# Second-layer token tiles placed between the block products of the next pair, and remainders of h computed a step later

## The chip, the core and the metric

The kernel runs on one core of a Trainium2 chip. Its engines work side by side, each through its own queue in order: TensorE (PE; its weight loads are listed as PEld), VectorE (DVE), ScalarE (ACT), GpSimd (POOL) and the engine that issues transfers (SP). The metric is the device time of one execution in microseconds (us).

## The reference

```python
x = attention(q, k, v)                  # window of 128 positions; 1152 tokens x 512
out = 0
for e in range(4):                      # four experts, 512 -> 1024 -> 512, every token
    h = np.maximum(x @ w1[e], 0.0)
    out += p[:, e:e + 1] * (h @ w2[e])
h = np.maximum(out @ w_in, 0.0)         # 512 -> 2048 -> 512
return h * h @ w_out
```

All is float32. The kernel splits each operand into a rounded high part and a remainder (`xh`, `xl`; `wh`, `wl`) and forms three products for each one: high by high, high by remainder, remainder by high.

## The kernel before

The work stands in the program in this order: attention; expert 0 and half of expert 1 (a planner sets the order, then a loop over items); the **pair stage**; and the last two weight matrices, handled as two more experts of 1024 (`e` of 4 and 5). An item is one slice of hidden features for one chunk of tokens. The change touches the pair stage, 20 items called pairs: the second half of expert 1 and experts 2 and 3, in slices `g` of 256 features, for two chunks of tokens (`PAIRS`). Chunk 0 has 2 x 256 tokens and chunk 1 has 2 x 320. The order is expert, then two slices, then chunk, then slice: (1,0,2), (1,0,3), (1,1,2), (1,1,3), (2,0,0) and so on, as (expert, chunk, slice). They are numbered 1 to 20 here.

`gemm1_pair` computes a pair's first layer as 2 x 2 blocks with seven block products instead of eight. Sums of weight blocks (`hs`, `ls`) and of token blocks (`ht`, `lt`, `hm`, `lm`) have been made ahead. A block product is six matmuls with 256 or 320 columns (2 parts of the contraction by 3), so a pair has 42. They accumulate in three PSUM tiles `pa`, `pb`, `pc`. Results of one product are read from PSUM before the next product is added to the same tile: DVE's `u2` reads `pb` after the second product, and the fifth product goes into `pb` again; `u3` reads it after the fifth, and the seventh goes into it.

`relu` makes the two parts of h for a quarter of the pair: ACT writes the high part, DVE the remainder (line 973). Three quarters come from sums c12, c21 (DVE) and c22 (POOL, line 1001).

`flush_one` computes the second layer of a pair that is pending. For each tile of 128 tokens (4 for chunk 0, 5 for chunk 1) `gemm2_pair` issues six matmuls with 512 columns into a `yacc` tile of PSUM. There are five such banks, taken in turn. After the second of two slices, `evac` (line 1063, DVE) adds each finished tile to y. In the main loop the flush of pair n-1 follows the seven products of pair n as one block:

```python
h = gemm1_pair(e, ch, f)
...
if len(pend) > (1 if two else LAG):
    flush_one()
```

`fill` is called between the products and between the tiles. It hands out steps of the background work on ACT, DVE and POOL: splitting later weights (line 347, and lines 199 to 214 for the last matrices, whose split is longer). `run_x2` transposes finished y tiles into the next `xh` and `xl`: four PE transposes into a PSUM tile of the `work` kind (the kind of `pa`, `pb`, `pc`; three banks in turn), an ACT copy (line 1082) and a DVE subtraction (line 1083). Before, one such tile follows each of the first four tiles of the flush of pair 19.

Of the kernel before, what the change touches and what calls it, by code (L numbers as in the profile page):

```python
# [13 lines left out]
ALU = mybir.AluOpType  # L14
# [116 lines left out]
def kernel(  # L131
# [814 lines left out]
    def gemm1_pair(e, ch, g):  # L946
# [23 lines left out]
        def relu(i, j, src):  # L970
            hh, hl = (x[:, j * n:(j + 1) * n] for x in h[i])
            nc.scalar.activation(out=hh, in_=src, func=ACTF.Relu)  # L972
            nc.vector.scalar_tensor_tensor(  # L973
                out=hl, in0=src, scalar=0.0, in1=f32(hh), op0=ALU.max, op1=ALU.subtract
            )

        p1, p5, u2, u3, c12, c21, c22 = (
            tmp(x) for x in ("p1", "p5", "u2", "u3", "c12", "c21", "c22")
        )
# [4 lines left out]
        add(u2, pb, p1)  # L984
        fill(0.6, step)
# [4 lines left out]
        relu(0, 0, pa)  # L990
        mm(pb, s3, f["t3"], False, False)
        add(u3, pb, p1)
        fill(0.6, step)
        mm(pc, s4, f["b22"], False, True)
        add(c12, pc, u2)
        relu(0, 1, c12)
        fill(0.6, step)
        mm(pb, a22, f["m4"], False, True)
        add(c21, pb, p1)
        relu(1, 0, c21)  # L1000
        nc.gpsimd.tensor_tensor(out=c22, in0=u3, in1=p5, op=ALU.add)  # L1001
        spent("POOL", 0.9)
        relu(1, 1, c22)
        fill(0.6, step)
        return h
# [138 lines left out]
    def flush_one():  # L1144
        e, ch, f, h, two = pend.pop(0)
        if two:
            first, last = f % 2 == 0, f % 2 == 1
        else:
            n = FT // 2 if e in (1, E) else FT
            first, last = f % n == 0, f % n == n - 1  # L1150
# [3 lines left out]
        for tile_ in ys[e, ch]:  # L1154
            if two:
                gemm2_pair(e, ch, f, h, tile_, first, last)
            else:
                gemm2(e, ch, f, h, [tile_], first, last)
            if last:
                evac(e, ch, [tile_], f, two)  # L1160
            elif two:
                run_x2()
            fill(1.0, 1.38 if two else 0.69)
        w_done(w2t, e, ch, f, two)
        if last:
            tiles = ys.pop((e, ch))
            if e == E - 1 and f == NQ - 1:
                x2todo.extend(PAIRS[ch][0] // P + i for i, _ in tiles)

# [390 lines left out]
    for it, (e, ch, f, two) in list(enumerate(items))[N1:]:  # L1560
# [8 lines left out]
        if two:  # L1569
            assert ch < len(PAIRS) - 1 or not xbg  # L1570
            h = gemm1_pair(e, ch, f)
# [8 lines left out]
        if two and not (pend or [(0, 0, 0, 0, two)])[0][4]:  # L1580
            while pend:
                flush_one()
# [11 lines left out]
        if len(pend) > (1 if two else LAG):  # L1594
# [43 lines left out]
```

## Time and profile before

| | us |
|---|---|
| median of three runs | 683.14 (683.11 to 684.08) |
| the profiled execution | 684.94 |
| its span, first to last instruction | 682.5 |
| pair stage in that span | 228.55 to 474.51 |
| PE busy in the span | 670.5 |

The profiled execution is 1.80 us above the median. Its span leaves out 2.44 us of its own time. The granted clock of TensorE was full in the whole pair stage.

### The profile page before, as it was taken

How to read it: one execution, taken by the hardware profiler on the slowest of the kernel's cores; microseconds unless marked ns; L12 is line 12 of the kernel's file. 1: busy time of each engine (PE TensorE's matmuls, PEld its weight loads, DVE VectorE, ACT ScalarE, POOL GpSimd, SP SyncE). 2: the span in 40 equal slices, each digit the busy share in tenths (PEclk: the TensorE clock that was granted, in tenths of full speed). 3: DMA queues.
4: the chain of work that ended last, by engine and by line, in shares of the span. 5: the costliest groups of instructions: out<-in, count | busy, mean ns of one | idle time of the engine just before them, and what ended most of it. 6: DMA issues, size and time to landing. Idle time of an engine off the chain costs nothing.

```text
span 682.5 us, 10267 instructions
## 1 busy us (share of the span) xinstructions
PE 670.5 (98%) x3792; PEld 596.8 (87%) x3792; DVE 415.4 (61%) x885; ACT 296.7 (43%) x697; POOL 286.5 (42%) x297
## 2 busy tenths in 40 slices
PE   8999999999999999999999999999999999999997
PEld 7777888889999898999899898888999999989996
DVE  4897898855556445444563557887777688742121
ACT  5798787633222323222323233333555544432221
POOL 2799996515443455334555433010322222222221
PEclk7999999999999999999999999999999999999999
DMA  7933222030300112101101203147204200001011
GB/s 204 280 104 96 70 77 62 11 124 31 122 5 29 32 32 93 62 32 40 54 32 61 63 1 124 61 162 259 74 4 168 76 0 1 1 1 47 1 46 46
DMA packets 37106, 47.60 MB, mean 70 GB/s; under 512 B 3392, under 2 KB 25408, under 8 KB 37056
## 3 DMA queue, kind: packets, MB, share of 16 engines
q1 hardware_dynamic: 37056, 46.95, 22.0%
q8 instruction: 29, 0.48, 0.3%
q14 instruction: 21, 0.17, 0.1%
HBM read 44.58 MB, written 2.36 MB: 69 GB/s over the span
## 4 chain that ended last, share of the span: by engine, by line
PE 87%; DVE 4%; POOL 3%; ACT 2%; issue 1%; SPq 1%; DMA 1%; POOLq 0%; ACTq 0%
PE hps L858 24%; PE yacc L1045 24%; PE yacc L1013 16%; PE hps L958 15%; PE xps L653 3%; PE tp L781 2%; PE sc L733 1%; POOL wl L422 1%; POOL ts L769 1%; DMA pt<-in_probs_dram 1%; PE hps L1454 1%; DVE y L1063 1%; SPq L1278 1%; POOL vl L422 1%; PE xtp L1078 1%
## 5 line engine op out<-in xcount | busy, mean ns | idle before, releaser
L1045 PE MATMUL yacc<-wh,hmem 128*128 128x512 f32 x488 | 165.8, 393 | 0.0
L1034 POOL TENSOR_TENSOR hmem<-r,hmem 128x384 fp32r<-128x384 f32 x48 | 53.1, 1106 | 161.1 <-ACT hmem L1033 158.9
L858 PE MATMUL hps<-xh,wh 128*128 128x384 f32 (+1 forms) x352 | 115.8, 329 | 0.0
L1013 PE MATMUL yacc<-wh,hmem 128*128 128x512 f32 x360 | 115.2, 391 | 0.0
L858 PE MATMUL hps<-xh,wl 128*128 128x384 f32 (+1 forms) x352 | 114.4, 325 | 0.4 <-DVE wl L347 0.4
L858 PE MATMUL hps<-xl,wh 128*128 128x384 f32 (+1 forms) x352 | 113.9, 324 | 0.0
L1045 PEld LDWEIGHTS yacc<-wh,hmem 128*128 128x128 f32 x488 | 91.6, 188 | 17.4
L1045 PE MATMUL yacc<-wl,hmem 128*128 128x512 f32 x244 | 96.2, 394 | 0.0
L1013 PEld LDWEIGHTS yacc<-wh,hmem 128*128 128x128 f32 x360 | 67.6, 188 | 13.5
L1013 PE MATMUL yacc<-wl,hmem 128*128 128x512 f32 x180 | 70.2, 390 | 0.0
L858 PEld LDWEIGHTS hps<-xh,wh 128*128 128x128 f32 x352 | 66.3, 188 | 3.6 <-issue 0.2
L858 PEld LDWEIGHTS hps<-xl,wh 128*128 128x128 f32 x352 | 66.3, 188 | 3.0 <-issue 0.2
L1032 DVE TENSOR_TENSOR r<-hps,r 128x384 f32<-128x384 f32 x48 | 26.7, 556 | 66.5 <-ACT r L1031 66.2
L858 PEld LDWEIGHTS hps<-xh,wl 128*128 128x128 f32 x352 | 66.2, 188 | 0.8 <-DVE wl L347 0.8
L1031 ACT ACTIVATE r<-hps 128x384 f32<-128x384 f32 x48 | 23.6, 492 | 90.0 <-PE hps L858 89.3
L1001 POOL TENSOR_TENSOR c<-u,p 128x256 f32<-128x256 f32 (+1 forms) x20 | 16.7, 833 | 104.1 <-DVE u L968 104.1
L1045 PEld LDWEIGHTS yacc<-wl,hmem 128*128 128x128 f32 x244 | 45.8, 188 | 7.4
L769 POOL TENSOR_SCALAR ts<-ts,st 128x256 f32<-128x256 f32 (+2 forms) x80 | 40.6, 521 | 26.8 <-DVE st L764 12.7
L973 DVE SCALAR_TENSOR_TENSOR hmem<-c,hmem 128x256 fp32r<-128x256 f32 (+1 forms) x60 | 37.8, 657 | 21.5 <-ACT hmem L972 21.5
L972 ACT ACTIVATE hmem<-c 128x256 fp32r<-128x256 f32 (+1 forms) x60 | 24.6, 439 | 60.6 <-DVE c L968 57.5
L347 POOL TENSOR_TENSOR wl<-wraw,wh 128x1024 fp32r<-128x1024 f32 x14 | 34.6, 2468 | 28.6 <-issue 14.5
L1063 DVE SCALAR_TENSOR_TENSOR y<-yacc,pt,y 128x512 f32<-128x512 f32 x54 | 38.8, 745 | 9.2 <-PE yacc L1013 6.5
(141 smaller groups left out, 1433.3 us busy)
## 6 DMA issues: line engine op xcount, KB each, us to landing
wraw<-in_w_dram SPq DMA_DIRECT2D x32, 512.0 KB, 3.9
wraw<-in_w_in_dram SPq DMA_DIRECT2D x16, 512.0 KB, 4.4
wraw<-in_w_out_dram SPq DMA_DIRECT2D x16, 512.0 KB, 4.1
rq<-in_qT_dram SPq DMA_DIRECT2D x8, 256.0 KB, 6.2
out_dram<-y SPq DMA_DIRECT2D x8, 256.0 KB, 2.1
rk<-in_kT_dram SPq DMA_DIRECT2D x8, 192.0 KB, 4.1
rv<-in_v_dram SPq DMA_DIRECT2D x8, 192.0 KB, 3.1
rq<-in_qT_dram SPq DMA_DIRECT2D x8, 192.0 KB, 2.6
```

The lines of the kernel that those rows point to most:

```text
L347: eng.tensor_tensor(out=lo[:, ks, :], in0=full, in1=f32(hi[:, ks, :]), op=ALU.subtract)
L769: nc.gpsimd.tensor_scalar(out=ts[0:n, g, :], in0=ts[0:n, g, :], scalar1=st[0:n, 2, g:g + 1], scalar2=1.0, op0=ALU.mult, op1=ALU.mult,)
L858: nc.tensor.matmul(out=ps, lhsT=l_[:, k, cs], rhs=r_[:, k, cols], start=(k == 0 and r_ is xh and l_ is wh and not second), stop=(k == KT - ...
L958: nc.tensor.matmul(out=ps, lhsT=a[l_][:, k, :], rhs=b[r_][:, k, :], start=start and k == 0 and l_ == r_, stop=stop and k == 1 and l_ == 1, ...
L972: nc.scalar.activation(out=hh, in_=src, func=ACTF.Relu)
L973: nc.vector.scalar_tensor_tensor(out=hl, in0=src, scalar=0.0, in1=f32(hh), op0=ALU.max, op1=ALU.subtract)
L1013: nc.tensor.matmul(out=y, lhsT=l_[:, ns], rhs=r_[:, fo, :], start=(first and fo == 0 and j == 0), stop=(last and fo == FTQ - 1 and j == 2),)
L1031: nc.scalar.activation(out=r, in_=ps, func=ACTF.Relu)
L1032: nc.vector.tensor_tensor(out=r, in0=ps, in1=r, op=ALU.mult)
L1034: nc.gpsimd.tensor_tensor(out=hl, in0=r, in1=f32(hh), op=ALU.subtract)
L1045: nc.tensor.matmul(out=y, lhsT=l_[:, ns], rhs=r_[:, fo, :], start=(first and j == 0), stop=(last and j == 2),)
L1063: nc.vector.scalar_tensor_tensor(out=yt, in0=y, scalar=pt[:, nt, e:e + 1], in1=yt, op0=ALU.mult, op1=ALU.add)
```

## The change

`flush_one` becomes a generator, `flush`, that stops after each token tile. `gemm1_pair` takes a function `tile_` and calls it after the fourth, fifth, sixth and seventh block product, so that a tile of the pending pair stands after each of these; a fifth tile follows behind the seventh product. The remainders are no longer computed at once: `relu` returns the DVE step, and it is given out later, the last one (c22) behind the next pair's `u2`. c22 itself is issued to POOL behind the sixth product instead of the seventh. `run_x2(2)` stands behind a pair in place of `run_x2()` behind each tile.

```diff
--- before.py
+++ after.py
@@ -943,7 +943,9 @@
             t3[:3] + [held(t3[3]), t3[4]],
         )
 
-    def gemm1_pair(e, ch, g):
+    held = []
+
+    def gemm1_pair(e, ch, g, tile_):
         n = PAIRS[ch][1]
         f = fx[ch]
         (ha, _), (hs, _), (la, _), (ls, _) = w1t[e, g]
@@ -970,38 +972,46 @@
         def relu(i, j, src):
             hh, hl = (x[:, j * n:(j + 1) * n] for x in h[i])
             nc.scalar.activation(out=hh, in_=src, func=ACTF.Relu)
-            nc.vector.scalar_tensor_tensor(
+            return lambda: nc.vector.scalar_tensor_tensor(
                 out=hl, in0=src, scalar=0.0, in1=f32(hh), op0=ALU.max, op1=ALU.subtract
             )
 
-        p1, p5, u2, u3, c12, c21, c22 = (
-            tmp(x) for x in ("p1", "p5", "u2", "u3", "c12", "c21", "c22")
-        )
+        p1, p5, u2, u3, c12, c21 = (tmp(x) for x in ("p1", "p5", "u2", "u3", "c12", "c21"))
         pa, pb, pc = (ps_tile("work", [P, n], "hps") for _ in range(3))
         mm(pa, a11, f["b11"], True, False)
         nc.scalar.activation(out=p1, in_=pa, func=ACTF.Copy)
         mm(pb, s2, f["t2"], True, False)
         add(u2, pb, p1)
+        while held:
+            held.pop(0)()
         fill(0.6, step)
         mm(pc, s1, f["t1"], True, False)
         nc.scalar.activation(out=p5, in_=pc, func=ACTF.Copy)
         fill(0.6, step)
         mm(pa, a12, f["b21"], False, True)
-        relu(0, 0, pa)
+        lo11 = relu(0, 0, pa)
+        tile_()
         mm(pb, s3, f["t3"], False, False)
         add(u3, pb, p1)
+        lo11()
         fill(0.6, step)
+        tile_()
         mm(pc, s4, f["b22"], False, True)
         add(c12, pc, u2)
-        relu(0, 1, c12)
+        lo12 = relu(0, 1, c12)
+        c22 = tmp("c22")
+        nc.gpsimd.tensor_tensor(out=c22, in0=u3, in1=p5, op=ALU.add)
+        spent("POOL", 0.9)
         fill(0.6, step)
+        tile_()
         mm(pb, a22, f["m4"], False, True)
         add(c21, pb, p1)
-        relu(1, 0, c21)
-        nc.gpsimd.tensor_tensor(out=c22, in0=u3, in1=p5, op=ALU.add)
-        spent("POOL", 0.9)
-        relu(1, 1, c22)
+        lo12()
+        lo21 = relu(1, 0, c21)
         fill(0.6, step)
+        tile_()
+        lo21()
+        held.append(relu(1, 1, c22))
         return h
 
     def gemm2_pair(e, ch, g, h, tile_, first, last):
@@ -1141,8 +1151,10 @@
         for _ in range(min(n, len(x2todo))):
             to_x2(x2todo.pop(0))
 
-    def flush_one():
+    def flush():
         e, ch, f, h, two = pend.pop(0)
+        while held:
+            held.pop(0)()
         if two:
             first, last = f % 2 == 0, f % 2 == 1
         else:
@@ -1158,14 +1170,23 @@
                 gemm2(e, ch, f, h, [tile_], first, last)
             if last:
                 evac(e, ch, [tile_], f, two)
-            elif two:
-                run_x2()
             fill(1.0, 1.38 if two else 0.69)
+            if tile_ is not ys[e, ch][-1]:
+                yield
         w_done(w2t, e, ch, f, two)
         if last:
             tiles = ys.pop((e, ch))
             if e == E - 1 and f == NQ - 1:
                 x2todo.extend(PAIRS[ch][0] // P + i for i, _ in tiles)
+        yield
+
+    def flush_one():
+        for _ in flush():
+            pass
+
+    def flush_all():
+        while pend:
+            yield from flush()
 
     def attn_close():
         if "w" not in late:
@@ -1568,7 +1589,11 @@
         quota["n"] = pace(it)
         if two:
             assert ch < len(PAIRS) - 1 or not xbg
-            h = gemm1_pair(e, ch, f)
+            rest_ = flush_all()
+            h = gemm1_pair(e, ch, f, lambda: next(rest_, None))
+            for _ in rest_:
+                pass
+            run_x2(2)
         else:
             if (e, ch, f) == (E, 0, 0):
                 late["top"].close()
@@ -1577,9 +1602,6 @@
                 while pend:
                     flush_one()
             h = gemm1(e, ch, f)
-        if two and not (pend or [(0, 0, 0, 0, two)])[0][4]:
-            while pend:
-                flush_one()
         pend.append((e, ch, f, h, two))
         w_done(w1t, e, ch, f, two)
         loads()
@@ -1591,7 +1613,7 @@
         else:
             quota["per"] = 1.0 + chunks(e)[ch][1] / P
             fill(1.0, 2.1)
-        if len(pend) > (1 if two else LAG):
+        if not two and len(pend) > LAG:
             flush_one()
     while bg or carry:
         bg_run()
```

PE in the fourth pair (320 columns), at the sixth and seventh block products (`hm`, `lm` are the operands of the seventh). Before:

```order
L958 MATMUL hps<-xl,hs 128x320
L958 MATMUL hps<-xh,ls 128x320
L958 MATMUL hps<-hm_2488,ha 128x320
L958 MATMUL hps<-lm_2489,ha 128x320
L958 MATMUL hps<-hm_2488,la 128x320
L958 MATMUL hps<-hm_2488,ha 128x320
L958 MATMUL hps<-lm_2489,ha 128x320
L958 MATMUL hps<-hm_2488,la 128x320
L1013 MATMUL yacc<-wh,hmem 128x512
L1013 MATMUL yacc<-wl,hmem 128x512
L1013 MATMUL yacc<-wh,hmem 128x512 x2
L1013 MATMUL yacc<-wl,hmem 128x512
```

With the change, at the same two products:

```order
L960 MATMUL hps<-xh,hs 128x320
L960 MATMUL hps<-xl,hs 128x320
L960 MATMUL hps<-xh,ls 128x320
L1023 MATMUL yacc<-wh,hmem 128x512
L1023 MATMUL yacc<-wl,hmem 128x512
L1023 MATMUL yacc<-wh,hmem 128x512 x2
L1023 MATMUL yacc<-wl,hmem 128x512
L1023 MATMUL yacc<-wh,hmem 128x512
L960 MATMUL hps<-hm_2488,ha 128x320
L960 MATMUL hps<-lm_2489,ha 128x320
L960 MATMUL hps<-hm_2488,la 128x320
L960 MATMUL hps<-hm_2488,ha 128x320
```

A tile of five rows (six matmuls) now stands between the two products, and each following tile has a product in front of it, where all tiles stood in one block.

DVE in the thirteenth pair (256 columns; it is the one whose flush ends a pass with five tiles), where `u` are the sums u2 and u3, `c` the sums c12 and c21, and `hmem` a remainder. Before:

```order
L968 TENSOR_TENSOR u_4057<-hps,p_4055 128x256
L973 SCALAR_TENSOR_TENSOR hmem<-hps,hmem 128x256
L968 TENSOR_TENSOR u_4058<-hps,p_4055 128x256
L968 TENSOR_TENSOR c_4059<-hps,u_4057 128x256
L973 SCALAR_TENSOR_TENSOR hmem<-c_4059,hmem 128x256
L968 TENSOR_TENSOR c_4060<-hps,p_4055 128x256
L973 SCALAR_TENSOR_TENSOR hmem<-c_4060,hmem 128x256
L973 SCALAR_TENSOR_TENSOR hmem<-c_4061,hmem 128x256
L1063 SCALAR_TENSOR_TENSOR y<-yacc,pt,y 128x512 x5
L968 TENSOR_TENSOR u_4171<-hps,p_4169 128x256
```

With the change, from this pair's u2 on:

```order
L970 TENSOR_TENSOR u_4047<-hps,p_4045 128x256
L975 SCALAR_TENSOR_TENSOR hmem<-c_4002,hmem 128x320
L1073 SCALAR_TENSOR_TENSOR y<-yacc,pt,y 128x512
L970 TENSOR_TENSOR u_4048<-hps,p_4045 128x256
L975 SCALAR_TENSOR_TENSOR hmem<-hps,hmem 128x256
L1073 SCALAR_TENSOR_TENSOR y<-yacc,pt,y 128x512
L970 TENSOR_TENSOR c_4049<-hps,u_4047 128x256
L1073 SCALAR_TENSOR_TENSOR y<-yacc,pt,y 128x512
L970 TENSOR_TENSOR c_4050<-hps,p_4045 128x256
L975 SCALAR_TENSOR_TENSOR hmem<-c_4049,hmem 128x256
L1073 SCALAR_TENSOR_TENSOR y<-yacc,pt,y 128x512
L975 SCALAR_TENSOR_TENSOR hmem<-c_4050,hmem 128x256
```

The five additions to y stand between the pair's own sums now; the second row is the remainder of the pair before, and the remainders of c12 and c21 come one step after their sums.

The transposes of y, PE around the first of them. Before, behind the seventh product of pair 20:

```order
L1013 MATMUL yacc<-wh,hmem 128x512
L1013 MATMUL yacc<-wl,hmem 128x512
L1013 MATMUL yacc<-wh,hmem 128x512 x2
L1013 MATMUL yacc<-wl,hmem 128x512
L1013 MATMUL yacc<-wh,hmem 128x512
L1078 MATMUL xtp<-ident,y 128x128 x4
L1013 MATMUL yacc<-wh,hmem 128x512
```

With the change, behind the seventh product of pair 19 (eight transposes, two tiles, and then pair 20 begins):

```order
L1023 MATMUL yacc<-wh,hmem 128x512
L1023 MATMUL yacc<-wl,hmem 128x512
L1023 MATMUL yacc<-wh,hmem 128x512 x2
L1023 MATMUL yacc<-wl,hmem 128x512
L1023 MATMUL yacc<-wh,hmem 128x512
L1088 MATMUL xtp<-ident,y 128x128 x8
L960 MATMUL hps<-xh,ha 128x320
L960 MATMUL hps<-xl,ha 128x320
```

The transposes moved from between tiles of a flush to the place between two pairs. DVE there with the change, from pair 19's c21 (second row, behind a split of weights) to pair 20's u2:

```order
L970 TENSOR_TENSOR c_4726<-hps,p_4721 128x320
L975 SCALAR_TENSOR_TENSOR hmem<-c_4725,hmem 128x320
L206 TENSOR_SCALAR wroom<-wroom 128x512
L1073 SCALAR_TENSOR_TENSOR y<-yacc,pt,y 128x512
L210 SCALAR_TENSOR_TENSOR wroom<-wraw_4608,wroom 128x512
L347 TENSOR_TENSOR wl<-wroom,wh 128x512
L975 SCALAR_TENSOR_TENSOR hmem<-c_4726,hmem 128x320
L1093 TENSOR_TENSOR xl<-xtp,xh 128x4x128 x2
L970 TENSOR_TENSOR u_4855<-hps,p_4853 128x320
```

Both subtractions of line 1093 (1083 before) stand behind what is left of pair 19 and ahead of pair 20's u2.

## Rows read from the trace of the kernel before

**Rows 1.** The page's part 4, the chain that ended last, by engine.

```profile
PE 87%; DVE 4%; POOL 3%; ACT 2%; issue 1%; SPq 1%; DMA 1%; POOLq 0%; ACTq 0%
```

**Rows 2.** Pair stage: us, busy PE, PEld, DVE, ACT, POOL; clock, DMA.

```profile
228.50:474.50 246.00, 244.48 (x1424) 220.56 (x1424) 139.66 (x256) 82.42 (x173) 95.76 (x82) 1.00 0.22 72
```

**Rows 3.** PE in time order, a pair with 256 columns: start us, us, instruction.

```profile
291.34 0.38 PE L958 MATMUL hps<-hm,ha 128*128 128x256 f32 x1
291.55 0.28 PE L958 MATMUL hps<-lm,ha 128*128 128x256 f32 x1
291.67 0.28 PE L958 MATMUL hps<-hm,la 128*128 128x256 f32 x1
```

**Rows 4.** PE in time order at its three longer waits, with what ended each.

```profile
326.42 0.28 PE L958 MATMUL hps<-xh,ls 128*128 128x256 f32 x1
326.96 0.39 PE L958 MATMUL hps<-hm,ha 128*128 128x256 f32 x1 [0.27 <-DVE u L968]
...
431.64 0.28 PE L958 MATMUL hps<-xh,la 128*128 128x256 f32 x1
432.49 0.39 PE L958 MATMUL hps<-xh,hs 128*128 128x256 f32 x1 [0.57 <-DVE u L968]
...
455.29 0.31 PE L958 MATMUL hps<-xh,la 128*128 128x320 f32 x1
456.28 0.41 PE L958 MATMUL hps<-xh,hs 128*128 128x320 f32 x1 [0.68 <-DVE u L968]
```

**Rows 5.** PE in time order: where two long second-layer runs begin and end.

```profile
245.00 0.40 PE L1013 MATMUL yacc<-wh,hmem 128*128 128x512 f32 x1
...
250.46 0.30 PE L958 MATMUL hps<-xh,ha 128*128 128x320 f32 x1
...
268.26 0.39 PE L1013 MATMUL yacc<-wh,hmem 128*128 128x512 f32 x1
...
275.09 0.28 PE L958 MATMUL hps<-xh,ha 128*128 128x256 f32 x1
275.20 0.28 PE L958 MATMUL hps<-xl,ha 128*128 128x256 f32 x1
```

**Rows 6.** PE in time order: a run of six, then one of nine.

```profile
149.06 0.39 PE L1045 MATMUL yacc<-wh,hmem 128*128 128x512 f32 x1
...
150.45 0.33 PE L858 MATMUL hps<-xh,wh 128*128 128x384 f32 x1
...
502.07 0.39 PE L1045 MATMUL yacc<-wh,hmem 128*128 128x512 f32 x1
...
504.15 0.33 PE L858 MATMUL hps<-xh,wh 128*128 128x384 f32 x1
```

**Rows 7.** DVE in time order ahead of the third of the longer waits.

```profile
453.88 0.74 DVE L1063 SCALAR_TENSOR_TENSOR y<-yacc,pt,y 128x512 f32<-128x512 f32 x1
454.54 0.68 DVE L210 SCALAR_TENSOR_TENSOR wroom<-wraw,wroom 128x512 int32<-128x512 int32 x1
455.14 0.68 DVE L347 TENSOR_TENSOR wl<-wroom,wh 128x512 fp32r<-128x512 f32 x1
455.74 0.48 DVE L968 TENSOR_TENSOR u<-hps,p 128x320 f32<-128x320 f32 x1
```

**Rows 8.** Line 1083, min/median/max ns; then PE in time order.

```profile
L1083 DVE TENSOR_TENSOR xl<-xtp,xh x9: 678/687/692, 462.3 to 493.5; 128x512 fp32r<-128x512 f32 x9
...
460.41 0.60 PE L1078 MATMUL xtp<-ident,y 128*128 128x128 f32 x4
460.76 0.47 PE L1013 MATMUL yacc<-wh,hmem 128*128 128x512 f32 x1
```

**Rows 9.** Line 347 on POOL in the pair stage; POOL and DVE from 341.

```profile
L347 POOL TENSOR_TENSOR wl<-wraw,wh 128x1024 fp32r<-128x1024 f32 x8 | 19.2, 2402 | 11.1 <-issue 11.0
...
341.08 2.40 POOL L347 TENSOR_TENSOR wl<-wraw,wh 128x1024 fp32r<-128x1024 f32 x1 [6.27 <-issue]
...
341.28 2.48 DVE L973 SCALAR_TENSOR_TENSOR hmem<-c,hmem 128x256 fp32r<-128x256 f32 x1 [0.49 <-ACT hmem L972]
```

## The prediction

> **What bounds the kernel now.** I read the chain that ended last first: 87% of it is PE [rows 1], so time comes or goes only where PE waits or works more. Then the pair stage by engine: of 246.00 us PE is busy 244.48, DVE 139.66, ACT 82.42, POOL 95.76, at full clock [rows 2]. What PE shows as idle is 1.52 us. A busy PE is not a PE at its pace, so I went through the starts of its matmuls in time order; the step from one start to the next is what a matmul costs.
>
> The steps are steady, 0.12 us for 256 columns, except where a product is added to a PSUM tile that DVE must read first. At the seventh product (operand hm) of a pair with 256 columns the first step is 0.21 in place of 0.12 [rows 3]: the sixth product, 6 x 0.12 = 0.72 us, is all the cover that DVE's u3 has. This stands in all ten such pairs. Pairs with 320 columns have more cover and lose nothing there. Three waits are longer, all for a sum u on DVE [rows 4]: 326.96 - 326.42 - 0.12 = 0.42; 432.49 - 431.64 - 0.12 = 0.73; 456.28 - 455.29 - 0.15 = 0.84. Ahead of the last, DVE does an addition to y, then two split steps of the last matrices, 0.66, 0.60 and 0.60 us after one another, and only then u2 [rows 7]: the five additions to y of the flush and the splits had piled up behind it. The rest of the stage runs without a gap.
>
> **What the change removes.** Three long waits, 0.42 + 0.73 + 0.84 = 1.99; the short ones, 10 x 0.09 = 0.9; and the slow first step after two of the long ones (the third is in the ten), 2 x 0.09 = 0.18. Together 3.1 us, 0.45% of the span, and this is the ceiling: PE's matmuls stay the same, and the stage has no other idle time. I expect nearly all of it back. A tile of six 512-column matmuls takes 1.39 us [rows 6]. With one behind the fourth product, the fifth waits for u2 only 0.72 + 0.72 + 1.39 = 2.8 us after the second product's end (1.4 before); with two around the sixth, the seventh has 1.39 + 0.72 + 1.39 = 3.5 us of cover for u3 (0.72 before). The backlog on DVE that made the long waits came from additions in a block; now one stands behind each tile. At the other end 2.6 us come back, if one of the two waits of the last stretch stays in half.
>
> **What it adds: switches.** Before, a pair has one run of second-layer matmuls; now it has four, so 3 x 20 = 60 more entries. A long run of 24 takes 250.46 - 245.00 = 5.46 us and one of 30 takes 275.09 - 268.26 = 6.83 [rows 5], so six more cost 1.37. A run of six by itself, behind other matmuls, takes 150.45 - 149.06 = 1.39 [rows 6]: about 0.025 more for an entry. Coming back to 256 columns the first step is 0.11 in place of 0.12 [rows 5], 0.005 to 0.01 back. I take 0.02 for an entry and return: 60 x 0.02 = 1.2 us. The other end is the run of nine in the last stage, 504.15 - 502.07 = 2.08 [rows 6] against 9 x 1.37/6 = 2.05, so at most 0.04 for an entry: 2.4 us. I take the low one, since that row is the same length, six.
>
> The Trainium skill, TensorE: Matmul & The Clock Gate, section Back-to-back issue gap, gives the gap between matmuls as a function of the column count alone (warm, 512 columns: 518 cycles, some 216 ns). The long run's 6.83/30 = 0.228 us is near to it, a short run's 0.232 is not that much. By that rule alone a switch is free and the sum is 1.2 us lower.
>
> **What it adds: transposes between two pairs.** Before, each y tile's transposes stand between second-layer tiles, and their four take 460.76 - 460.41 = 0.35 us [rows 8]; that cost only moves. But now two of them, eight transposes, stand right between pairs 19 and 20, in the banks that pair 20's second and third products want next. The second product so waits for the first subtraction of line 1083 on DVE, and u2 stands behind both. From the end of pair 19's seventh product: PE does a tile (1.39), the transposes (0.70) and the first product of pair 20 (6 x 0.147 = 0.88), and wants the bank at 2.97. DVE does c21 and a remainder, about 0.4 each by u2's row, and a shorter split step; the fourth addition to y can't start before its tile ends, at 1.5 with the way, and takes 0.66 (2.15); two split steps of 0.60 (3.35) [rows 7]; the remainder of c21, 0.4 (3.75); and the subtraction, 0.69 [rows 8]: 4.45. PE waits 1.5 us; DVE comes to this place about 0.1 late, since the third addition to y and a split step lie ahead of c21. I take 1.6. Bounds: 0.4 if the two split steps have been done by then, 2.6 if one more engine's turn (ACT's copies stand behind a split and the high part of c22) is waited for. The other two transposes, behind pair 20, are followed by five tiles (6.8 us) that use no such bank: nothing.
>
> **At nothing.** The remainders: the same count and length on DVE, and each is needed later than it is given. The tightest is c21's: the last matmul of the next pair's first tile reads it, 1.39 + 4 x 0.72 + 5 x 0.23 = 5.4 us behind the seventh product; DVE reaches it at 1.5 + 0.66 + 0.4 = 2.6, or 3.8 with two split steps. Without this cover each 1 us late is 1 us of PE in each pair. The pending pair's second-layer weights are wanted three products earlier, 2.2 us, and in the timeline of before every split of them is done well ahead of that. The additions to y: five banks, and a bank is taken again a whole tile run later. c22 on POOL: ACT's high part of it stands ahead of the next pair's p1, but c22 is issued one product and two tiles earlier. Freed weight buffers: the flush ends where the pair ends, in both programs, so loads on SP are released at the same time. Nothing is queued behind them that is not now.
>
> **Sum.** - 3.1 + 1.2 + 1.6 = - 0.3 us. The profiled span of 682.5 would become 682.2; the profiled execution, at 684.94, is 1.80 above the median of 683.14, and I take the same difference on the median: 682.8 us. What a measurement tells from no change is about 0.2%, 1.4 us.
>
> **Rivals.**
> 1. Switches are free: - 3.1 + 1.6 = - 1.5: 681.6; with the wait for the transposes at its low end, 0.4, - 2.7: 680.4. For it: the long run's step is steady from its sixth matmul on, and products of 256 columns come back at full pace. Against: the row of the run of six. The Trainium skill's section Back-to-back issue gap (TensorE: Matmul & The Clock Gate) would give this one.
> 2. Switches cost 0.04 each, as in the last stage: - 3.1 + 2.4 + 1.6 = + 0.9: 684.0, and 685.0 with the transposes at 2.6. Against it: it is read from a run of another length.
> 3. Slower: a remainder is held by POOL. At 341.28 a remainder took 2.48 us, beside POOL's 2.40 at 341.08; eight such steps are in the stage [rows 9]. It is 2.06 above its usual 0.42, and the cover of c21's remainder is 5.4 - 2.6 = 2.8: one hold is covered, two in a row (4.1) put PE 1.3 late. From two such places on the kernel is slower: - 0.3 + 2.6 = + 2.3, 685.4. Against it: two of POOL's long steps must follow each other just there, and the stretch with much DVE work comes after the last of them. The Trainium skill, GPSIMD Engine Reference, section Specifications, says that GpSimd shares its SBUF interfaces with VectorE and contends with instructions of two SBUF inputs, which a remainder of a c is; the trace agrees, by the 2.48.
> 4. The change doesn't do what it says: DVE stays late, as each sum now stands behind an addition to y that waits for a tile. Then nothing comes back: + 1.2 + 1.6 = + 2.8, 685.9. Against it: the covers of 2.8 and 3.5 us above.
>
> **Chances and range.** Forecast 0.50 (of it, 0.43 within 0.2%, 0.04 faster, 0.03 slower), rival 1 0.27 (0.19 faster, 0.08 within), rival 2 0.13 (half within, half slower), rival 3 0.05, rival 4 0.05. Faster 0.23, same 0.57, slower 0.20. The forecast's own range: - 3.1 + 1.2 + 0.4 = - 1.5 to - 2.6 + 1.2 + 2.6 = + 1.2, 681.6 to 684.3. The range goes on to rival 1 with part of its low end and to the slower two: 681.1 to 685.4.
>
> **What would show it.** In the changed profile: PE's waits for u gone from the list, and the seventh product's first step at 0.12; tiles of six at 1.39 between products; between pairs 19 and 20 PE waiting 1 to 2 us for the subtraction behind the transposes; the stage shorter by about 0.3 us. Wrong it would be by tiles at 1.37 or at 1.45, by no wait behind the transposes, or by PE waiting for a remainder (hmem) at the last matmul of a tile.

## The result: slower by half a per cent, and the profile after

The changed kernel takes 686.92 us (median of six, 685.76 to 688.70) beside 683.61 us for the kernel before on the same chip: a ratio of 1.0051, 95% interval 1.0033 to 1.0069. In a later set of executions it was 687.67 beside 683.54, 1.0061 (1.0049 to 1.0074). The forecast was 682.8 with a range up to 685.4. It was counted from 683.14, the median of the first three of these six executions of the kernel before; so 0.47 us of the distance is that baseline, and the rest, a loss of 3.3 us where 0.3 was to be gained, is the change.

The profiled execution took 688.70 us with a span of 686.9. Its pair stage runs from the first matmul of pair 1 to the first of the last two matrices:

```profile
228.85 0.28 PE L960 MATMUL hps<-xh,ha 128*128 128x256 f32 x1
...
477.93 0.33 PE L858 MATMUL hps<-xh,wh 128*128 128x384 f32 x1
```

That is 249.08 us, 3.12 more than the 245.96 of before (228.55 to 474.51). The same stretch as [rows 2], with the same columns, and then pieces of its end:

```profile
228.85:477.93 249.08, 246.11 (x1425) 221.16 (x1423) 144.94 (x252) 80.92 (x171) 93.18 (x82) 0.99 0.19 65
...
450.00:457.50 7.50, 5.43 (x34) 4.68 (x33) 6.94 (x14) 3.69 (x8) 0.00 (x0) 1.00 0.80 280
457.50:460.70 3.20, 3.20 (x14) 3.20 (x13) 1.83 (x4) 0.44 (x1) 0.00 (x0) 0.50 0.00 0
460.70:478.00 17.30, 17.30 (x87) 14.73 (x87) 12.73 (x23) 5.54 (x11) 0.88 (x1) 0.99 0.48 166
```

PE is idle for 2.97 us and not for 1.52, and the clock column is new: from 457.5 to 460.7 the granted clock is 0.50, TensorE's level of 1.2 GHz, while PE is busy without a gap. PE's waits from 228 to 500 us, by engine and line: us in total, times, longest. (These are PE's idle times. Below, as in the prediction, a wait is the step from one start to the next, less the usual step, which comes out some 0.2 us longer.)

```profile
PE hps L960 <- DVE xl L1093: 2.1, 1, 2.1
PE hps L960 <- DVE u L970: 0.9, 1, 0.9
PE hps L858 <- DVE xl L1093: 0.7, 1, 0.7
```

None of the three waits of [rows 4] is among them. Pairs 3 to 19 run as forecast: no wait, tiles of six at 1.38 to 1.39 us, the seventh product's first step at 0.12 (284.95 to 285.07) in place of the 0.21 of [rows 3]. In their place stand three waits at the edges: in pair 2, between pairs 19 and 20, and behind the stage. In PE's order of time:

```profile
244.08 0.39 PE L1023 MATMUL yacc<-wh,hmem 128*128 128x512 f32 x1
245.37 0.39 PE L960 MATMUL hps<-xh,hs 128*128 128x256 f32 x1 [0.90 <-DVE u L970]
...
450.87 0.39 PE L1023 MATMUL yacc<-wh,hmem 128*128 128x512 f32 x1
...
452.26 1.20 PE L1088 MATMUL xtp<-ident,y 128*128 128x128 f32 x8
453.21 0.39 PE L960 MATMUL hps<-xh,ha 128*128 128x320 f32 x1
...
454.02 0.31 PE L960 MATMUL hps<-xh,la 128*128 128x320 f32 x1
456.40 0.41 PE L960 MATMUL hps<-ht,hs 128*128 128x320 f32 x1 [2.07 <-DVE xl L1093]
...
457.55 0.47 PE L960 MATMUL hps<-lt,hs 128*128 128x320 f32 x1
457.81 0.47 PE L960 MATMUL hps<-ht,ls 128*128 128x320 f32 x1
...
485.38 0.60 PE L1088 MATMUL xtp<-ident,y 128*128 128x128 f32 x4
486.70 0.44 PE L858 MATMUL hps<-xh,wh 128*128 128x384 f32 x1 [0.72 <-DVE xl L1093]
```

The first is 245.37 - 244.08 - 0.23 = 1.06 us. The second is 456.40 - 454.02 - 0.15 = 2.23 us, and at 457.55 a matmul takes 0.26 to the next start in place of 0.15: the slow clock. The third is 486.70 - 485.38 - 0.35 = 0.97 us, with the 0.35 of four transposes in [rows 8].

**Where DVE was, in pair 2.** DVE in time order, and the POOL step beside it:

```profile
240.65 2.36 DVE L975 SCALAR_TENSOR_TENSOR hmem<-c,hmem 128x256 fp32r<-128x256 f32 x1 [1.22 <-ACT hmem L974]
242.93 2.06 DVE L1073 SCALAR_TENSOR_TENSOR y<-yacc,pt,y 128x512 f32<-128x512 f32 x3
244.91 0.41 DVE L970 TENSOR_TENSOR u<-hps,p 128x256 f32<-128x256 f32 x1
```

```profile
240.32 2.41 POOL L347 TENSOR_TENSOR wl<-wraw,wh 128x1024 fp32r<-128x1024 f32 x1 [1.17 <-ACT wh L345]
```

The remainder of c22 of pair 1 waits 1.22 us for ACT and then takes 2.36 us beside POOL's 2.41; three additions to y and u2 are queued behind it. It stands there because the flush of the items ahead of pair 1 empties `held` first, so this remainder, alone among them, comes ahead of the next pair's u2.

**Where DVE was, between pairs 19 and 20.** DVE in time order:

```profile
451.27 0.74 DVE L1073 SCALAR_TENSOR_TENSOR y<-yacc,pt,y 128x512 f32<-128x512 f32 x1
451.93 0.42 DVE L203 TENSOR_SCALAR wroom<-wraw 128x512 int32<-128x512 int32 x1
452.26 0.48 DVE L970 TENSOR_TENSOR c<-hps,p 128x320 f32<-128x320 f32 x1
452.66 0.48 DVE L975 SCALAR_TENSOR_TENSOR hmem<-c,hmem 128x320 fp32r<-128x320 f32 x1
453.06 0.42 DVE L206 TENSOR_SCALAR wroom<-wroom 128x512 f32<-128x512 f32 x1
453.40 0.75 DVE L1073 SCALAR_TENSOR_TENSOR y<-yacc,pt,y 128x512 f32<-128x512 f32 x1
454.06 0.68 DVE L210 SCALAR_TENSOR_TENSOR wroom<-wraw,wroom 128x512 int32<-128x512 int32 x1
454.66 0.69 DVE L347 TENSOR_TENSOR wl<-wroom,wh 128x512 fp32r<-128x512 f32 x1
455.26 0.49 DVE L975 SCALAR_TENSOR_TENSOR hmem<-c,hmem 128x320 fp32r<-128x320 f32 x1
455.66 1.28 DVE L1093 TENSOR_TENSOR xl<-xtp,xh 128x512 fp32r<-128x512 f32 x2
```

The subtraction that PE waits for, L1093, begins at 455.66, so the first of the two is done at about 456.35, with the 0.69 us of [rows 8]. PE begins the tile behind pair 19's seventh product at 450.87.

**Where DVE was, behind the stage.** DVE in time order in the changed kernel, then in the kernel before:

```profile
484.95 1.09 DVE L347 TENSOR_TENSOR wl<-wroom,wh 128x512 fp32r<-128x512 f32 x1 [1.11 <-ACT wh L345]
485.97 0.68 DVE L1093 TENSOR_TENSOR xl<-xtp,xh 128x512 fp32r<-128x512 f32 x1
```

```profile
484.37 1.09 DVE L347 TENSOR_TENSOR wl<-wroom,wh 128x512 fp32r<-128x512 f32 x1 [1.11 <-ACT wh L345]
485.38 0.68 DVE L1083 TENSOR_TENSOR xl<-xtp,xh 128x512 fp32r<-128x512 f32 x1
```

A split step (L347) waits 1.11 us for ACT's wh, and the subtraction into xl stands behind it. The kernel before has the same row, with the same 1.11 us, but one item later, at 484.37, where second-layer tiles stand behind each first layer; there it costs PE nothing.

The whole difference of the spans, 686.92 - 682.47 = 4.45 us, is then 0.30 ahead of the stage (whose start lies between 227.3 and 228.9 us in these profiles, whatever the kernel), 3.12 in it, 1.04 from its end to the last matmul (204.73 and 203.69 us), and nothing in the tail. What each part of it is due to is read from the experiments.

### The profile page after: what moved, and what is told of

Read it like the earlier page. It is cut to its first block, busy times and chain, and to the rows that moved or that the text cites. A ratio compares the mean times of both kernels' runs of the same rounds, so it can differ in the third digit from the quotient of the medians.

```text
span 686.9 us, 10258 instructions
## 1 busy us (share of the span) xinstructions
PE 674.3 (98%) x3792; PEld 599.8 (87%) x3792; DVE 421.5 (61%) x885; ACT 296.7 (43%) x697; POOL 283.6 (41%) x297
## 3 DMA queue, kind: packets, MB, share of 16 engines
HBM read 44.58 MB, written 2.36 MB: 68 GB/s over the span
## 4 chain that ended last, share of the span: by engine, by line
PE 86%; DVE 4%; ACT 3%; POOL 3%; issue 1%; DMA 1%; SPq 1%; POOLq 0%; ACTq 0%; DVEq 0%
PE hps L858 24%; PE yacc L1055 23%; PE yacc L1023 17%; PE hps L960 15%; PE xps L653 2%; PE tp L781 2%; PE sc L733 1%; POOL wl L422 1%; DMA pt<-in_probs_dram 1%; SPq L1299 1%; POOL ts L769 1%; DVE y L1073 1%; ACT wh L416 1%; DVE wl L347 1%; PE hps L1475 1%
## 5 line engine op out<-in xcount | busy, mean ns | idle before, releaser
L1055 PE MATMUL yacc<-wh,hmem 128*128 128x512 f32 x488 | 166.3, 393 | 0.0
L1023 PE MATMUL yacc<-wh,hmem 128*128 128x512 f32 x360 | 124.6, 392 | 0.0
L975 DVE SCALAR_TENSOR_TENSOR hmem<-c,hmem 128x256 fp32r<-128x256 f32 (+1 forms) x60 | 47.2, 789 | 2.4 <-ACT hmem L974 1.8
L970 DVE TENSOR_TENSOR u<-hps,p 128x256 f32<-128x256 f32 (+1 forms) x40 | 18.3, 457 | 46.3 <-PE hps L960 45.6
```

The costliest lines, as they stand in the source:

```text
L970: nc.vector.tensor_tensor(out=out, in0=x, in1=y, op=ALU.add)
L975: return lambda: nc.vector.scalar_tensor_tensor(out=hl, in0=src, scalar=0.0, in1=f32(hh), op0=ALU.max, op1=ALU.subtract)
L1023: nc.tensor.matmul(out=y, lhsT=l_[:, ns], rhs=r_[:, fo, :], start=(first and fo == 0 and j == 0), stop=(last and fo == FTQ - 1 and j == 2),)
L1055: nc.tensor.matmul(out=y, lhsT=l_[:, ns], rhs=r_[:, fo, :], start=(first and j == 0), stop=(last and j == 2),)
```

## The experiments

Waits are those from 228 to 500 us. Lengths of the pair stage and of what lies behind it (first matmul of the last two matrices to the last matmul of all) come from each kernel's one profile. Each median is beside executions of the kernel before on the same chip, medians of 683.63, 683.49 and 683.54 us for the three sets.

| kernel | median us | ratio (95%) | stage | behind it | PE's waits of over 0.3 us |
|---|---|---|---|---|---|
| before | | | 245.96 | 203.69 | 0.42, 0.73, 0.84 u |
| changed | 686.92 | 1.0051 (1.0033-1.0069) | 249.08 | 204.73 | 1.06 u, 2.23 xl, 0.97 xl; half clock |
| a_x2_late | 683.69 | 1.0004 (0.9995-1.0013) | 245.11 | 204.72 | 1.05 u, 0.97 xl |
| a_held_on | 685.82 | 1.0031 (1.0019-1.0044) | 246.35 | 204.74 | 2.22 xl, 0.94 xl |
| a_both | 682.43 | 0.9986 (0.9977-0.9995) | 243.94 | 204.75 | 0.96 xl |
| b_x2_early | 686.39 | 1.0040 (1.0028-1.0053) | 249.31 | 203.69 | 0.42, 0.73 u, 0.41 y, 2.42 xl; half clock |
| a_both_phase | 682.11 | 0.9979 (0.9970-0.9988) | 243.94 | 203.72 | none |
| a_at_once | 682.32 | 0.9983 (0.9974-0.9992) | 243.94 | 204.74 | 1.03 xl |
| b_held | 682.17 | 0.9984 (0.9975-0.9993) | 243.40 | 204.75 | 1.02 xl |
| a_filled | 686.01 | 1.0034 (1.0021-1.0047) | 247.51 | 204.78 | 1.06 u, 0.97 xl |
| b_held_phase | 681.17 | 0.9964 (0.9952-0.9977) | 243.39 | 203.68 | none |
| b_last_held | 683.78 | 1.0005 (0.9996-1.0014) | 245.97 | 203.66 | 0.43, 0.74, 0.85 u |
| b_order | 684.66 | 1.0014 (1.0006-1.0023) | 245.49 | 204.72 | 0.42, 0.42, 0.77 u, 1.01 xl |
| a_again | 687.67 | 1.0061 (1.0049-1.0074) | 249.06 | 204.72 | 1.06 u, 2.23 xl, 0.97 xl; half clock |

**The transposes moved away (a_x2_late).** Labels with a_ start from the changed kernel, in those with b_ the token tiles of a pair stay in one block, as in the kernel before.

```diff
-            run_x2(2)
...
             if last:
                 evac(e, ch, [tile_], f, two)
+            if (e, ch, f, two) == (E - 1, 1, NQ - 1, True):
+                run_x2()
```

> The changed kernel, with one edit: run_x2(2) behind pairs 19 and 20 is taken out, and one transposed tile follows each of the first four token tiles of pair 20, which stand alone at the end of the stage. Theory A (the place of the transposes costs most of the loss: in the profile after, TensorE waits 2.2 us for the subtraction into xl between pairs 19 and 20, and for about 3 us behind that wait it runs at a granted clock of 0.50, some 1.5 us more): about 3.9 us under the changed kernel, some 683.0 us, no wait between pairs 19 and 20, and the granted clock 1.00 there. Rival B (the transposes only carry their wait with them, since DVE is as late behind pair 20): the wait stands at the end of the stage, and the time falls by less than 1 us. Rival C (the loss is in the 60 further switches and the held remainders, and the profile's half clock is an accident of that one execution): the time falls by 2.3 us, the wait alone, to some 684.6.

683.69 us: 3.2 under the first median of the changed kernel, 4.0 under the second. The stage is 249.08 - 245.11 = 3.97 us shorter, the wait is gone, and it doesn't come back behind pair 20. B falls. The time lies between A's 683.0 and C's 684.6; the stage, and a granted clock that stays at 1.00 there, speak for A.

**Pair 1's remainder behind pair 2's u2 (a_held_on), and both edits (a_both).**

```diff
     def flush():
         e, ch, f, h, two = pend.pop(0)
-        while held:
+        while two and held:
             held.pop(0)()
```

> The changed kernel, with one edit: a remainder that is held is not given out ahead of the flush of an item that is no pair, so that the last remainder of pair 1 comes behind the u2 of pair 2, as everywhere else. In the profile after it stands on DVE ahead of three additions to y and of u2, waits 1.22 us for ACT and takes 2.36 us beside a POOL subtraction of 2.41 us; TensorE then waits 0.90 us for u2. Theory A (those 3.6 us on DVE are why u2 is late): the wait in pair 2 goes and the time falls by 0.9 to 1.2 us, to some 685.8. Rival B (u2 would be late anyway, since the three additions to y end only then): the wait stays within 0.3 us, and the time is that of the changed kernel, 686.9.

> Both edits together: the transposes behind the token tiles of pair 20, and the remainder of pair 1 behind the u2 of pair 2. Theory A (the two losses are of places apart, and add up): 3.9 + 1.1 us under the changed kernel, some 681.9 us, which is 1.6 us under the kernel before; what is left is the 3.1 us recovered less some 1.2 us for the switches. Rival B (an extra 60 switches and the later remainders eat what the waits gave): 683.5, the same as the kernel before. Rival C (the half clock of the profile was an accident): 683.5 as well, but with the waits of before gone and the medians of the other kernels spaced by 2.3 rather than 3.9 us.

The first gives 685.82, 1.1 lower, and the wait in pair 2 is gone: theory A. Its profile holds a finding besides. Its wait between pairs 19 and 20 is the same, but the clock stays full behind it; PE in time order, then windows:

```profile
451.55 0.31 PE L960 MATMUL hps<-xh,la 128*128 128x320 f32 x1
453.92 0.42 PE L960 MATMUL hps<-ht,hs 128*128 128x320 f32 x1 [2.06 <-DVE xl L1093]
454.18 0.32 PE L960 MATMUL hps<-lt,hs 128*128 128x320 f32 x1
```

```profile
453.92:457.00 3.08, 3.08 (x20) 3.04 (x21) 2.37 (x5) 0.57 (x2) 0.00 (x0) 1.00 0.31 122
457.00:460.50 3.50, 3.50 (x20) 3.02 (x19) 1.38 (x4) 1.38 (x3) 0.70 (x1) 1.00 0.00 0
```

So the wait and the slow clock can be told apart: from the changed kernel to this one the stage loses 249.08 - 246.35 = 2.73 us. The same edit takes 245.11 - 243.94 = 1.17 us off a_x2_late's stage, which has no slow clock; that is pair 2's part, and 2.73 - 1.17 = 1.56 us is left for the clock. Both edits together give 682.43, 1.2 us under the kernel before, with an interval that lies below 1. The two losses add up as theory A has it: its stage is 249.08 - 243.94 = 5.14 us shorter, 3.97 with the first edit and 1.17 more with the second; the 1.17 holds the wait's 1.06 and slower steps behind it. The time is 0.5 over theory A's 681.9.

**The place of the transposes alone (b_x2_early).**

```diff
-            elif two:
-                run_x2()
...
             flush_one()
+        if two:
+            run_x2(2)
```

> The kernel before, with one part of the change alone: two transposed tiles behind pair 19's work and two behind pair 20's (run_x2(2)), in place of one behind each token tile of pair 19. Nothing else is changed. Theory A (the place alone makes the loss, whatever stands around it): TensorE waits some 2 us for xl between pairs 19 and 20, the granted clock may fall to 0.50 behind it, and the time is 2.3 to 3.9 us over the kernel before, 685.9 to 687.5. Rival B (the wait comes from DVE's load with token tiles between the products, which the kernel before does not have there): a wait of under 1 us, full clock, and a time within 1 us of the kernel before.

686.39: moving this one call makes a kernel with nothing interleaved 2.8 us slower. PE waits 2.42 us for xl, and behind it the clock falls again. Theory A holds, and rival B falls: the wait needs no token tiles between the products.

**PE kept busy in the wait (a_filled), and the changed kernel again (a_again).**

```diff
         nc.scalar.activation(out=p1, in_=pa, func=ACTF.Copy)
+        if (e, ch, g) == (E - 1, 1, NQ - 1):
+            idle_ = ps_tile("y", [P, DM], "yacc")
+            for _ in range(9):
+                nc.tensor.matmul(out=idle_, lhsT=ha[:, 0, :], rhs=w2t[e, g - 1][0][0][:, 0, :], start=True, stop=True)
         mm(pb, s2, f["t2"], True, False)
```

> The changed kernel with one addition: nine matmuls of 512 columns into an otherwise unused bank, some 2.05 us, between the first and the second product of pair 20, where TensorE waits 2.2 us for xl. Their result is not used. Theory A (the half clock behind the wait, 3.4 us at 0.50 in two of three profiles with that wait, comes from TensorE's idleness): the clock stays at 1.00, the restart of the second product stays where it was (within 0.2 us), the executions stop falling into two groups some 1.5 us apart, and the median falls by 0.5 to 1.6 us, to 685.3 to 686.4. Rival B (the half clock has nothing to do with the wait): the groups stay, the time is 686.9 or, if the matmuls delay the second product, more.

> The changed kernel, unaltered, for more of its executions beside those of the version with the filled wait (spans 683.7 to 684.4 us). Theory A (behind the wait of 2.2 us for xl the clock falls in some executions, for 1.6 us more): spans in two groups, around 684.3 and around 686.0, and if the profiled one is of the long group its clock is 0.50 for some 3 us behind the wait, if of the short group 1.00. Rival B (the fall is not what makes its executions spread): all within 0.6 us of each other.

PE in time order in the filled kernel, then its window:

```profile
453.06 0.31 PE L960 MATMUL hps<-xh,la 128*128 128x320 f32 x1
453.21 2.23 PE L986 MATMUL yacc<-wh,ha 128*128 128x512 f32 x9
455.43 0.42 PE L960 MATMUL hps<-ht,hs 128*128 128x320 f32 x1
```

```profile
456.00:460.00 4.00, 4.00 (x26) 3.74 (x26) 1.83 (x4) 1.95 (x4) 0.00 (x0) 1.00 0.12 47
```

The second product starts 455.43 - 453.06 = 2.37 us behind the first one's last matmul, against 456.40 - 454.02 = 2.38 without the nine: they cost nothing. The clock stays at 1.00, and the stage is 249.08 - 247.51 = 1.57 us shorter, though PE does more work: nearly the 1.56 found above for the clock. The median is in theory A's range, 0.9 under the changed kernel's first and 1.7 under its second. The changed kernel, run again, has the slow clock in its profile:

```profile
456.00:459.40 3.40, 3.40 (x15) 3.40 (x14) 1.83 (x4) 0.44 (x1) 0.00 (x0) 0.50 0.04 14
```

Its five spans are 685.6 to 687.1 us, so the short one of theory A's two groups is missing here; the first six executions had three of 684.0 to 684.5 and three of 685.7 to 686.9. The filled kernel's six are 683.7 to 684.4, and with the clock at 1.00 a_filled's rival B falls. For a_again neither side holds in full: the spread of 1.5 us is over rival B's 0.6, but no short execution of the changed kernel was profiled, and that the clock parts its two groups isn't shown. Of four profiles with the bare wait, three show the slow clock behind it and one (a_held_on) doesn't. The Trainium skill (TensorE: Matmul & The Clock Gate, section What's actually happening) says that the slow clock is the default and that activity releases it; the filled wait agrees. Why one execution kept its clock through the same wait isn't shown.

**One background step fewer (a_both_phase).** At the first item behind the stage, on top of a_both:

```diff
                 while pend:
                     flush_one()
+                quota["left"] -= 1.0
```

> The version with both repairs (transposes behind pair 20's tiles, pair 1's last remainder behind pair 2's u2), with one edit: the allowance of the background work is made one step smaller at the first item after the pair stage. In the two-repair version TensorE waits 0.7 us there for xl at the third item, because DVE stands 1.11 us in an L347 step that waits for ACT; in the kernel before, the same L347 step falls on the fourth item, which has token tiles around it, and costs nothing. Theory A (the 1.0 us lost after the stage are only the phase in which the background steps come): the wait goes, the time from the stage's end to the last instruction falls from 209.0 to 208.0 us, and the time is 0.8 to 1.0 us under the two-repair version, some 681.5 us. Rival B (another background step takes its place, or the order at the stage's end was not the cause): the wait stays or moves, and the time is within 0.3 us of 682.4.

The wait for xl is gone, and the stretch behind the stage is 204.75 - 203.72 = 1.03 us shorter, as theory A has it. The median fell by 0.3 only, to 682.11, beside a kernel before that was 0.14 lower in that set. That is the time of rival B, so the gain is shown by the profile, not by the median.

**The two halves of the change apart (a_at_once, b_held).** In a_at_once each `relu` gives its remainder out at once and c22 stands behind the seventh product, with the tiles between the products and the transposes behind pair 20's tiles, as in a_both. In b_held the tiles stay in one block, one transposed tile follows each of the first four tiles of pair 19 as before, c22 stays behind the sixth product, and the remainders are held:

```diff
-            h = gemm1_pair(e, ch, f, lambda: next(rest_, None))
+            h = gemm1_pair(e, ch, f, lambda: None)
             for _ in rest_:
                 pass
-            run_x2(2)
...
         e, ch, f, h, two = pend.pop(0)
-        while held:
+        while held and (e, ch, f) == (E - 1, 1, NQ - 1):
             held.pop(0)()
...
             if last:
                 evac(e, ch, [tile_], f, two)
+            elif two:
+                run_x2()
```

> The interleaving alone: the changed kernel with the transposes behind pair 20's tiles, all four remainders of a pair computed at once, and c22 behind the seventh product, as in the kernel before. Theory A (the token tiles between the products keep DVE from falling behind, so the later remainders add nothing): the waits for u stay away, and the time is that of the two-repair version, 682.4 within 0.5 us (no remainder is held, so pair 2 has no wait of 1 us either). Rival B (the later remainders are what keeps u2, u3 and c12 on time, since DVE waits some 0.54 us for ACT ahead of each remainder given out at once): waits for u of 0.3 to 0.8 us come back at several pairs, and the time is 1 to 2 us higher, 683.5 to 684.5.

> The later remainders alone: the order of the kernel before (all token tiles of a pair in one block behind the seven products, transposes between the tiles of pair 19), with the remainders given out a step later, the last one behind the next pair's u2, and c22 behind the sixth product. Theory A (the long waits for u of the kernel before come from additions to y and background steps behind the block of tiles, which stay): two or three waits of 0.4 to 0.8 us for u remain, at most 0.5 us is gained, 683.1 to 683.6 us. Rival B (the remainders in DVE's queue were what made u late): the waits go without any further switch, 3 us are gained, and the time is 680.5 to 681 us.

The first went as theory A has it: 682.32, no wait for u. The second contradicts it. With no tile moved, all three long waits for u are gone; rival B's mechanism holds, though its time was too low by the wait behind the stage and a little more. The reason stands in what DVE itself waits for. First among DVE's waits from 228 to 475 us, in the kernel before; then the row of the same wait in b_held; then that of a_at_once:

```profile
DVE hmem L973 <- ACT hmem L972: 49.0, 59, 1.8
```

```profile
DVE hmem L975 <- ACT hmem L974: 1.6, 4, 0.6
```

```profile
DVE hmem L975 <- ACT hmem L974: 51.3, 59, 3.8
```

Before, DVE stood still 59 times, 49.0 us in all, ahead of a remainder whose high part ACT had not yet written. Given out a step later the remainder finds it there: 1.6 us in all. In a_at_once DVE waits as much as before, but with a tile between the products PE doesn't notice. Either half is enough for the long waits. The short ones differ: in b_held the seventh product of the ten pairs with 256 columns still begins with 0.18 to 0.19 us (290.01 to 290.20) in place of 0.12, some 0.65 us in all, and in a_both it doesn't. Since a_both's stage is even so 0.54 us longer than b_held's, its 60 more switches cost an estimated 0.54 + 0.65 = 1.2 us, the price forecast for them. With the remainders held, the tiles between the products cost more than they give.

**Only the last remainder (b_last_held), and only the order of the main loop (b_order).** The changed kernel runs a pair's flush ahead of the freeing of buffers, the loads and the new step allowance (`quota["per"]`); before, it came behind them. b_order is the kernel before with that alone; b_last_held is the kernel before, order included, with c22's remainder alone put into `held`:

```diff
-        if two and not (pend or [(0, 0, 0, 0, two)])[0][4]:
+        if two:
             while pend:
                 flush_one()
         pend.append((e, ch, f, h, two))
...
-        if len(pend) > (1 if two else LAG):
+        if not two and len(pend) > LAG:
             flush_one()
```

> The kernel before with the smallest part of the later remainders: only the last remainder of a pair (from c22) is given out behind the next pair's u2; the others at once, c22 behind the seventh product, tiles in one block, and the order of the main loop as before. Theory A (the remainder of c22, which waits for POOL and ACT, is what stands in DVE's queue at the wrong moment): the three long waits for u go, and the time is 1 to 1.5 us under the kernel before, some 682.3 us. Rival B (the long waits come from additions to y and background steps behind the block, and their phase decides): at least two waits of 0.4 to 0.9 us remain and the time is 683.2 to 683.8 us.

> The kernel before, with nothing held and nothing interleaved; only the block of token tiles stands before the bookkeeping of the main loop (the freeing of weight buffers, the loads and the new allowance per step) instead of behind it, as it does in the changed kernel. That shifts by a step or so where the background steps fall on DVE. Theory A (the waits for u and for xl depend on which background step falls there, so a shift alone moves them): the long waits for u of the kernel before change place or go, the wait of 0.7 to 0.9 us for xl behind the stage appears, and the time is anywhere within 1.5 us of the kernel before. Rival B (the waits come from the remainders' place): the waits for u stay within 0.3 us of 0.42, 0.73 and 0.84 at the same pairs, and the time is 683.5 within 0.4 us.

b_last_held changes nothing: the same three waits, 683.78 us. DVE still waits 40.3 us for ACT there, ahead of the other remainders, so theory A falls: holding c22's alone is not enough. (b_held also issues c22 to POOL a product earlier; that was not tried by itself.) b_order is 1.1 us slower than the kernel before (684.66). Two of its waits for u stay where they were, so rival B holds for these; one stands elsewhere (at 373 us in place of 432), and the wait of 1.01 for xl behind the stage is there, as theory A has it: the 1.03 us behind the stage come from the order of the bookkeeping, not from tiles or remainders. Against b_order, its like, b_held gains 245.49 - 243.40 = 2.09 us of stage and 2.5 us of median.

**The version to keep (b_held_phase):** b_held with the one-step edit of a_both_phase.

> The later remainders alone (token tiles of a pair in one block, as in the kernel before), with the background work's allowance one step smaller at the first item after the pair stage. The version without that edit has a pair stage of 243.40 us (245.96 before), no waits for u, and behind the stage a wait of 0.8 us for xl. Theory A (the same phase as in the two-repair version, where this edit took 1.02 us off the stretch behind the stage): 203.7 us from the stage's end to the last matmul instead of 204.75, and a time 0.8 to 1.0 us lower, 681.2 to 681.4 us, some 2.2 us under the kernel before. Rival B (the phase is another here): the wait stays, 682.2 us.

681.17 us, 2.4 under the kernel before, with no wait of over 0.3 us in the pair stage or just behind it. It has the lowest median of these kernels, and it puts no token tile between the products.

## Why the prediction was wrong, step by step

- **"What the change removes", with "switches": net - 3.1 + 1.2 = - 1.9 us.** Right: with the new waits taken away (a_both) the stage is 243.94 - 245.96 = - 2.02. But the reason given was half of it. The working put the backlog on DVE down to additions in a block, which the interleaving spreads. It left out DVE's 49.0 us of standing before ACT's high parts and put the later remainders "at nothing", so it did not see that they alone remove the long waits and make the stage 2.56 us shorter (b_held, 245.96 - 243.40; 2.09 beside its like, b_order), more than the two halves together.
- **"Transposes between two pairs", 1.6 us, bounds 0.4 to 2.6.** The mechanism was there; the wait was 2.23, and the place cost 246.35 - 243.94 = 2.41 at full clock (a_held_on beside a_both). The prediction had DVE come to this place 0.1 late and be done 4.45 us behind the seventh product. In the profile c21 starts 452.26 - 450.87 = 1.39 us behind it, after the addition to y and the split step that were priced at 0.1, and the first subtraction ends at 5.5. The backlog of one microsecond that DVE brings to this place is what was mis-sized. PE wants the bank at 3.3, not at 2.97: eight transposes take 0.95 between pairs, not 0.70.
- **The clock.** No term had it, and it is the step that failed worst: a PE wait was priced at its own length. It cost 1.56 us more, and with the 2.41 the place of the transposes costs 3.97, more than the change gives.
- **Rival 3, a remainder held by POOL.** Remainders were held often: nine of those of a sum c take 2.1 to 2.7 us in the stage, each beside a POOL step of 2.4 to 2.7, and at 415.96 two in a row take 4.74. Where the rival had PE wait, at a tile's last matmul, it never does. One hold cost something, the one in pair 2 (2.36 us beside POOL's 2.41, behind the wait of 1.22 for ACT), and through u2: 1.17 us. It was given 5 in 100 and two places as a condition; one place, with a remainder ahead of the u2 that PE waits for, was enough for a loss. The Trainium skill (GPSIMD Engine Reference, section Specifications) says that GpSimd contends with DVE instructions of two SBUF inputs; the trace agrees, as the same form takes 0.41 us at 443.01 with POOL idle.
- **"At nothing".** The flush's new place in the main loop was looked at for loads only. It also shifts the background steps by one, and that is the 1.04 us behind the stage.

The terms of the stage, measured: - 2.02 + 1.17 + 2.41 + 1.56 = + 3.12. As differences of stages they must add up; the clock's 1.56 has a check of its own in a_filled's 1.57.

## What to carry to other kernels

Look at what the late engine itself waits for before spreading its work: a step that stands idle for another engine's result can be issued one step later, if nothing that is waited for is queued behind its new place (in pair 2 something was). A wait of TensorE can cost more than its length: behind a wait of 2.2 to 2.4 us, matmuls ran at half clock in three of four profiles here. Such a place is to be avoided, or filled with work. And when background work is dealt out by a running count, moving a call past the bookkeeping moves every later step: test that shift alone, as a control.

## What was not expected of the hardware

The same wait, 2.2 us long, was followed by more than 3 us at a granted clock of 0.50 in two profiles of the changed kernel and by full clock in a_held_on's. The fall didn't come at once: in the changed kernel PE resumes at 456.40 at full pace, and the slow steps begin at 457.55. Nine matmuls, whose result nobody uses, made the pair stage 1.57 us shorter by keeping TensorE at work there.
